# The loads of q, k and v asked for one at a time: an order of transfers on one queue of a fused attention and expert kernel

## Chip, core and metric

The kernel runs on one core of a Trainium2 chip. The metric is the device time in microseconds (us) of one execution, and lower is better. The core has five engines with their own instruction streams: PE multiplies matrices, DVE and ACT work on tiles elementwise, POOL does elementwise work and indirect transfers, and SP here only issues direct transfers (DMAs) between HBM and on-chip memory.

## What is computed

The input is q, k and v of 8 batches, 8 heads, 576 positions and 64 columns. Two attentions are added, one over means of four neighbours and one over a band of seven positions, and the sum goes through a layer of eight experts of which each token takes one:

```python
q_d, k_d, v_d = (x.reshape(B, H, S // 4, 4, D).mean(axis=3) for x in (q, k, v))
out = np.repeat(sm_attn(q_d, k_d, v_d), 4, axis=2)          # sm_attn: softmax(q k^T / 8) v
mask = np.abs(pos[:, None] - pos[None, :]) < 4
out += softmax(np.where(mask, q @ k^T / 8, -1e9)) @ v
x = out as 4608 tokens of 512;  e = argmax(x @ w_gate + modality_bias[modality_id])
result[token] = p_e * (relu(x[token] @ w1[e]) @ w2[e])
```

## The kernel before

The attention stage runs in 32 steps, step n being two pairs of heads of batch n // 4. A table, `PHASE` (line 61), gives each operation of a step a position in units of a step: operation x of step n stands at n + PHASE[x]. `build` collects all of them as calls with a position (`call`, line 1250), sorts them (line 1346) and writes them out in that order under a manual schedule, so that every engine gets its instructions in the order of the positions. A step lasts some 7 us.

Loads are calls in the same list. `load_qk` (line 226) fills a tile `qt` and a tile `kt` for half a batch, that is for the steps 2h and 2h + 1 of half h; each tile is rotated over three buffers, and each is filled by two transfers of 288 KB (line 244). The first three halves use another layout (lines 237 and 239). PE reads the tiles first in the transposes `tp` (line 298) at position 2h. The call stands at 2h - 5 + 0.4 (line 1274), just behind the transposes of step 2h - 5, the last readers of the buffer. `load_v` (line 250) fills `vw`, of which there are two, one per batch in turn. Eight transfers of 180 KB fill one: four for heads 0 to 3 (part 0) and four for heads 4 to 7 (part 4). Lines 1269 to 1272 place the two clusters of four at positions 4b + 2.84 and 4b + 3.64 for batch b + 1, those of the last batch earlier. PE reads part 0 first in `vp` (line 279) of step 4b + 4, at position 4b + 6.44, and part 4 two steps later.

All of these are issued by SP, which also issues the stores of the attention's result (`xs`, line 639, in fours) and the loads of the first expert's weights (`raw`, line 854). SP takes its instructions strictly in order. Each transfer counts up one of eight semaphores in turn, and before it issues one SP waits for the landing of the transfer eight places earlier. The first load into a reused `qt` or `kt` also waits for PE to have left the buffer, and the first of four stores for DVE. Nothing on SP waits for a time: a position is only a place in its order.

After the attention, from about 251 us, PE multiplies the tokens with the experts' weights until the end.

Of the kernel before, what the change touches and what calls it, by code (L numbers as in the profile page):

```python
# [19 lines left out]
B, H, S, D = 8, 8, 576, 64  # L20
# [31 lines left out]
NHOLD = 8  # L52

QUADS = 3


SPLIT = {4: (2, 1, 1), 2: (2,), 1: (2,)}
# [141 lines left out]
class Attention:  # L199
# [23 lines left out]
        for j in range(2):  # L223
            (nc.vector, nc.gpsimd)[j].memset(s.vw[j], 0.0)

    def load_qk(s, b, half):
        nc = s.nc

        qt = s.ld.tile([128, 9, 2, D], F32, name="qt", bufs=3)
        kt = s.ld.tile([128, 9, 2, D], F32, name="kt", bufs=3)  # L230
        s.QK[2 * b + half] = (qt, kt)
        if 2 * b + half < QUADS:
            for g in (0, 2, 1):
                for t, src in ((qt, s.q), (kt, s.k)):
                    h = src[b, 4 * half : 4 * half + 4].rearrange("(a y) s d -> a (y s) d", a=2)
                    if g == 2:
                        nc.sync.dma_start(t[:, 4], h[:, 512:640].rearrange("a p d -> p a d"))
                    else:
                        nc.sync.dma_start(s.quads(t, g), h[:, 640 * g : 640 * g + 512].rearrange("a (p x) d -> p a (x d)", x=4))
            return  # L240
        for t, src in ((qt, s.q), (kt, s.k)):
            for a in range(2):
                h = src[b, 4 * half + 2 * a : 4 * half + 2 * a + 2].rearrange("h s d -> (h s) d")
                nc.sync.dma_start(t[:, :, a], h.rearrange("(j p) d -> p j d", p=128))

    def quads(s, t, g):

        return t[:, 5 * g : 5 * g + 4].rearrange("p j a d -> p (j a d)").rearrange("p (a x) -> p a x", a=2)

    def load_v(s, b, part, W=4):  # L250
        nc = s.nc
        vw = s.vw[b % 2]


        vf = s.v.rearrange("b h s d -> (b h s) d")
        N = H * NB
        for j in (0, 2, 1, 3):
            lo = S * H * b + SUB * j - PAD
            n0, n1 = NB * part, NB * part + NB * W
            if lo + n0 * BLK < 0:  # L260
                nc.sync.dma_start(vw[PAD:KEYS, 0], vf[0 : KEYS - PAD])
                n0 = 1
            if lo + n1 * BLK > B * H * S:
                n1 = N - 1
                t = lo + n1 * BLK
                nc.sync.dma_start(vw[32 * j : 32 * j + min(KEYS, B * H * S - t), n1], vf[t : min(t + KEYS, B * H * S)])
            nc.sync.dma_start(vw[32 * j : 32 * j + KEYS, n0:n1],
                              vf[lo + n0 * BLK : lo + n1 * BLK].rearrange("(n x) d -> x n d", x=BLK)[:KEYS])
# [17 lines left out]
    def tp(s, n, nm):  # L286

        src = s.QK[n // 2]["qk".index(nm)]
        p = s.t["tp", nm, n] = s.ps.tile([128, 512], F32, name="tp", tag="T", bufs=TB)
        if n // 2 < QUADS:  # L290
            t = s.quads(src, n % 2)
# [786 lines left out]
class Large:  # L1078
# [4 lines left out]
    W = {"1": (0, 0), "2": (0, 1), "5": (1, 0), "6": (1, 0), "7": (1, 0), "4": (1, 1), "3": (0, 1)}  # L1083
# [117 lines left out]
def build(tc, q, k, v, mid, w_gate, bias, w1, w2, out):  # L1201
    nc = tc.nc
    with ExitStack() as ctx:
# [10 lines left out]
        with ExitStack() as actx:  # L1214
# [7 lines left out]
            at = Attention(tc, actx, ectx, C, ps, q, k, v)  # L1222
# [27 lines left out]
            def call(at, f, *args):  # L1250
                calls.append((at, len(calls), f, args))
# [3 lines left out]
            last = max(P["tpq"], P["tpk"], P["tpt"])  # L1255
            used = max(P["avl0"], P["avl1"])
# [3 lines left out]
            for nm, p in P.items():  # L1260
                f, i = (nm[:-1], int(nm[-1])) if nm[-1].isdigit() and nm not in ("ch1", "ch2") else (nm, 0)
# [6 lines left out]
            for b in range(B):  # L1268
                if b + 1 < B:
                    for j in range(2):  # L1270
                        late_ = (1.39, 0.78)[j] if b == B - 2 else 0
                        call(4 * b - 1 + used + 0.3 + 0.8 * j - late_, at.load_v, b + 1, 4 * j)
            for h in range(3, N // 2):
                call(2 * h - 5 + last + 0.25, at.load_qk, h // 2, h % 2)


            for j in range(3):
# [51 lines left out]
            T, R, E, W = {}, {}, {}, []  # L1329
            t = 4 * (EB - 1) + max(P[x] for x in P if x[:2] == "st") + 0.02  # L1330
# [46 lines left out]
            with tc.high_priority():  # L1377
                last = range(B - 2, B)
# [194 lines left out]
        with tc.For_i(0, nu, 1) as iv:  # L1573
# [7 lines left out]
            W = [moe.chunk(e, c) for c in range(8)]  # L1581
# [31 lines left out]
```

## Time and profile before

| | us |
|---|---|
| median of 3 runs | 666.24 |
| lowest and highest | 661.93 and 669.0 |
| the profiled execution | 670.8 |
| its span, first to last instruction | 669.1 |

The profiled execution lasts 1.7 us longer than its span. PE is busy for 634.6 us of the span (95%), DVE for 439.7, ACT for 386.9 and POOL for 340.9. A busy share is an average over stages of different kinds, so the stages have to be read apart.

### The profile page before, as it was taken

The page shows a single profiled execution, that of the slowest core. Times are in us where ns is not written, and L with a number is a line of the kernel's source. Part 1 is how long each engine was busy: PE and PEld are TensorE (multiplying, and loading weights), DVE is VectorE, ACT ScalarE, POOL GpSimd, SP SyncE. Part 2 cuts the span into 40 slices and gives each one's busy share as a digit, 9 for nine tenths or more (in the row PEclk, how much of TensorE's full clock was granted, in tenths as well). Part 3 has the DMA queues.
Part 4 walks back from the last instruction along what each step waited for, and adds up shares of the span by engine and source line. Part 5 has one row for each costly group of instructions (what it writes and reads, how often), then busy time and mean ns, then how long its engine had stood idle before and what let it go on. Part 6 is the DMA issues. An engine that isn't in the chain of part 4 may idle for free. (4 is left out here: it accounts for less than half of the span.)

```text
span 669.1 us, 16362 instructions
## 1 busy us (share of the span) xinstructions
PE 634.6 (95%) x6099; PEld 498.9 (75%) x6099; DVE 439.7 (66%) x912; ACT 386.9 (58%) x870; POOL 340.9 (51%) x378
## 2 busy tenths in 40 slices
PE   8889999998999979999999999999999999999995
PEld 5666666766676656887888788888888888889794
DVE  7678898989989685853356672758548765236610
ACT  4688889987998883313454732448144473245610
POOL 7533646635565963245059776498774820141211
PEclk9799999998999999999999999999999999999999
DMA  7999997899778924379112425134341335449300
GB/s 187 201 185 193 168 183 139 178 196 175 172 153 168 188 88 157 77 138 235 43 45 94 107 83 161 49 103 107 97 148 68 102 95 161 146 135 287 135 14 31
DMA packets 168859, 90.21 MB, mean 135 GB/s; under 512 B 131812, under 2 KB 153354, under 8 KB 168778
## 3 DMA queue, kind: packets, MB, share of 16 engines
q1 hardware_dynamic: 160810, 69.96, 48.2%
q0 software_dynamic: 7968, 19.18, 9.2%
q8 instruction: 49, 0.80, 0.6%
q14 instruction: 32, 0.26, 0.2%
HBM read 69.86 MB, written 19.51 MB: 134 GB/s over the span
## 5 line engine op out<-in xcount | busy, mean ns | idle before, releaser
L1062 PE MATMUL l<-V,H 128*128 128x512 f32 x792 | 187.2, 394 | 0.0
L1062 PEld LDWEIGHTS l<-V,H 128*128 128x128 f32 x792 | 148.0, 188 | 33.9
L948 POOL DMA_INDIRECT xg<-xs,m x64 | 76.2, 1191 | 19.2 <-issue 18.9
L426 POOL TENSOR_TENSOR le<-le,zr 128x384 f32<-128x384 f32 x32 | 26.6, 830 | 93.6 <-DVE zr L422 42.2
L1072 POOL DMA_INDIRECT out_dram<-o,tq x24 | 27.8, 1157 | 76.8 <-ACT o L1064 52.1
L442 ACT COPY Pw<-lt 32x288 f32<-32x288 f32 x128 | 54.7, 427 | 6.9 <-DVE lt L437 5.0
L1008 PE MATMUL l<-X,H 128*128 128x512 f32 (+1 forms) x240 | 54.2, 375 | 0.5 <-ACT o L1064 0.5
L1064 ACT ACTIVATE o<-l,tq 128x512 f32<-128x512 f32 x24 | 16.5, 689 | 60.9 <-issue 27.6
L645 POOL DMA_INDIRECT tab<-ig,si x36 | 36.3, 1007 | 28.5 <-DVE mni L667 21.7
L1008 PEld LDWEIGHTS l<-X,H 128*128 128x128 f32 x240 | 41.5, 188 | 9.0 <-ACT o L1064 1.0
L1165 ACT ACTIVATE H<-o 128x512 fp32r<-128x512 f32 x36 | 22.8, 634 | 39.0 <-DVE o L1187 30.4
L481 PE MATMUL avl<-Pw,vw 128*64 128x96 f32 x768 | 40.2, 251 | 5.5 <-ACT Pw L442 4.5
L331 ACT COPY kT<-tp 64x512 f32<-64x512 f32 x64 | 37.1, 580 | 7.2 <-PE tp L294 3.0
L481 PEld LDWEIGHTS avl<-Pw,vw 128*64 128x64 f32 x768 | 33.4, 136 | 10.5 <-ACT Pw L442 6.2
L1014 DVE SCALAR_TENSOR_TENSOR H<-l,H 128x512 fp32r<-128x512 f32 x24 | 16.2, 687 | 34.8 <-ACT H L1013 31.4
L885 DVE TENSOR_TENSOR V<-raw,V 128x1024 fp32r<-128x1024 f32 x22 | 32.9, 1520 | 7.7 <-ACT V L879 6.8
L412 ACT ACTIVATE de<-scd,dm 128x144 f32<-128x144 f32 x96 | 36.1, 379 | 1.9
L1072 POOL DMA_INDIRECT out_dram<-o,tg x10 | 11.3, 1133 | 50.7 <-ACT o L1064 35.7
L373 PE MATMUL sc<-kT,qT 128*24 128x64 f32 x1536 | 35.8, 226 | 0.8 <-ACT kT L331 0.8
L373 PEld LDWEIGHTS sc<-kT,qT 128*24 128x24 f32 x1536 | 25.1, 105 | 14.4 <-issue 10.3
L1013 ACT ACTIVATE H<-l 128x512 fp32r<-128x512 f32 x24 | 13.8, 596 | 35.6 <-PE l L1008 25.4
L492 DVE TENSOR_TENSOR X<-avl,Od 128x224 f32<-128x224 f32 (+1 forms) x64 | 26.5, 430 | 7.4 <-PE avl L481 2.5
(283 smaller groups left out, 1444.2 us busy)
## 6 DMA issues: line engine op xcount, KB each, us to landing
raw<-in_moe_w_dram SPq DMA_DIRECT2D x112, 128.0 KB
raw<-in_moe_w_dram SPq DMA_DIRECT2D x28, 512.0 KB
vw<-in_v_dram SPq DMA_DIRECT2D x60, 180.0 KB
qt<-in_q_dram SPq DMA_DIRECT2D x26, 288.0 KB
kt<-in_k_dram SPq DMA_DIRECT2D x26, 288.0 KB
xs<-R SPq DMA_DIRECT2D x48, 128.0 KB
xs<-G SPq DMA_DIRECT2D x16, 128.0 KB
qt<-in_q_dram SPq DMA_DIRECT2D x6, 256.0 KB
```

Of the source, the lines that this page charges most:

```text
L331: s.nc.scalar.copy(s.kB[r, g, a, PAD + 64 * g : PAD + 64 * g + 512], p[r])
L373: s.nc.tensor.matmul(p[32 * j : 32 * j + SUB, 2 * i : 2 * i + 2, :], qT[:, q0 : q0 + SUB], kB[:, :, q0 : q0 + WIN], start=False, stop=(i = ...
L412: s.nc.scalar.activation(x, s.t["scd", n][:, c].rearrange("p (k x) -> p k x", k=NB), AF.Exp, bias=m[:, c : c + 1], accum_out=s.t["z", n][: ...
L426: s.nc.gpsimd.tensor_tensor(e, e, z[:, : 2 * NB].unsqueeze(2).broadcast_to([128, 2 * NB, WIN]), op=ALU.mult)
L442: s.nc.scalar.copy(s.Pw[n % NPW][r, :, j, :SUB], s.t["lt", n][r, :, :SUB])
L481: s.nc.tensor.matmul(p[64 * a : 64 * a + 64, c], vw[:, NB * (4 * (hp // 2) + hp % 2 + 2 * a) + k, :], Pw[:, 2 * k + a], start=True, stop=T ...
L645: i = nc.gpsimd.indirect_dma_start(out=s.tab[:, :], out_offset=bass.IndirectOffsetOnAxis(ap=C.si[:, t : t + 1], axis=0), in_=C.ig[:, t, :] ...
L885: (nc.gpsimd if turn == 4 else nc.vector).tensor_tensor(lo, raw, hi.bitcast(F32), op=ALU.subtract)
L948: s.nc.gpsimd.indirect_dma_start(out=R[l].rearrange("p h (i x) -> p (h i) x", i=4)[:, i, :], out_offset=None, in_=s.xs.rearrange("n (a x) ...
L1008: nc.tensor.matmul(p[:, f % n, :], a[:, fs], x[:, k, :N], start=(k == 0 and i == 0), stop=(k == 3 and i == 2))
L1062: nc.tensor.matmul(p, l, x[:, f % 2, :], start=(f == 0 and i == 0), stop=(f == 7 and i == 2))
L1072: nc.gpsimd.indirect_dma_start(out=s.out[:, :], out_offset=bass.IndirectOffsetOnAxis(ap=T[:, h, 0:1], axis=0), in_=o, in_offset=None, boun ...
```

## The change

The four transfers of a half of q and k become four calls, half a step apart, in the order q, k, q, k of their index `part` taken as (first pair of q, second pair of q, first of k, second of k). v's eight transfers become eight calls: 0.4 of a step apart, with the second four 1.6 steps behind the first four, so that all eight are evenly spaced. For the last batch v's positions stay. The first transfer of each group keeps its position, and the tiles, the sizes and every other engine's order stay as they were.

```diff
+QKGAP, VGAP = 0.5, (0.4, 1.6)
...
+        if part:
+            return s.load_heads(b, half, part)
...
-        for t, src in ((qt, s.q), (kt, s.k)):
-            for a in range(2):
-                h = src[b, 4 * half + 2 * a : 4 * half + 2 * a + 2].rearrange("h s d -> (h s) d")
-                nc.sync.dma_start(t[:, :, a], h.rearrange("(j p) d -> p j d", p=128))
+        s.load_heads(b, half, 0)
+
+    def load_heads(s, b, half, part):
+
+        a, x = part % 2, part // 2
+        h = (s.q, s.k)[x][b, 4 * half + 2 * a : 4 * half + 2 * a + 2].rearrange("h s d -> (h s) d")
+        s.nc.sync.dma_start(s.QK[2 * b + half][x][:, :, a], h.rearrange("(j p) d -> p j d", p=128))
...
-    def load_v(s, b, part, W=4):
+    def load_v(s, b, part, W=4, js=(0, 2, 1, 3)):
...
-        for j in (0, 2, 1, 3):
+        for j in js:
...
-                        call(4 * b - 1 + used + 0.3 + 0.8 * j - late_, at.load_v, b + 1, 4 * j)
+                        for i, x in enumerate((0, 2, 1, 3)):
+                            call(4 * b - 1 + used + 0.3 + (0.8 if b == B - 2 else VGAP[1]) * j - late_ + (0 if b == B - 2 else VGAP[0]) * i,
+                                 at.load_v, b + 1, 4 * j, 4, (x,))
             for h in range(3, N // 2):
-                call(2 * h - 5 + last + 0.25, at.load_qk, h // 2, h % 2)
+                for i in range(4):
+                    call(2 * h - 5 + last + 0.25 + QKGAP * i, at.load_qk, h // 2, h % 2, i)
```

Only SP's order changes. In the middle of the stage, round the loads of half 12 (`qt_2907`, `kt_2908`) and of v for batch 5 (`vw1`), SP has this before:

```order
L267 DMA vw1_155<-in_v_dram 30x24x64 x4
L639 DMA xs_66<-R_2600 32x8x128 x4
L244 DMA qt_2907<-in_q_dram 128x9x64 x2
L244 DMA kt_2908<-in_k_dram 128x9x64 x2
L267 DMA vw1_155<-in_v_dram 30x24x64 x4
L639 DMA xs_66<-R_3029 32x4x128 x4
L639 DMA xs_66<-R_2823 32x8x128 x4
```

And this now (`qt_2905`, `kt_2906`; lines six higher):

```order
L273 DMA vw1_155<-in_v_dram 30x24x64
L250 DMA qt_2905<-in_q_dram 128x9x64
L273 DMA vw1_155<-in_v_dram 30x24x64
L250 DMA qt_2905<-in_q_dram 128x9x64
L273 DMA vw1_155<-in_v_dram 30x24x64
L250 DMA kt_2906<-in_k_dram 128x9x64
L273 DMA vw1_155<-in_v_dram 30x24x64
L645 DMA xs_66<-R_3022 32x4x128 x4
L273 DMA vw1_155<-in_v_dram 30x24x64
L645 DMA xs_66<-R_2822 32x8x128 x4
L250 DMA kt_2906<-in_k_dram 128x9x64
L273 DMA vw1_155<-in_v_dram 30x24x64
```

Two loads of v have moved in among those of q and k, and the second transfer of k has moved behind eight stores. Near the end of the stage, the loads of the last half 15 (`qt_3896`, `kt_3897`) stand, before the change, ahead of the second chunk of weights (`raw0`; the rows ISA work out an address):

```order
L244 DMA qt_3896<-in_q_dram 128x9x64 x2
L244 DMA kt_3897<-in_k_dram 128x9x64 x2
L267 DMA vw1_155<-in_v_dram 30x24x64 x4
L854 ISA
L854 DMA raw0_3709<-in_moe_w1_dram 32x1024
L854 ISA
L854 DMA raw0_3709<-in_moe_w1_dram 32x1024
L854 ISA
L854 DMA raw0_3709<-in_moe_w1_dram 32x1024
L854 ISA
L854 DMA raw0_3709<-in_moe_w1_dram 32x1024
L267 DMA vw1_155<-in_v_dram 30x24x64
```

Now only one transfer of q is left there, and the last transfer of v for batch 6 (`vw0`) comes behind four of batch 7 (`vw1`):

```order
L250 DMA qt_3895<-in_q_dram 128x9x64
L273 DMA vw1_155<-in_v_dram 30x24x64 x4
L273 DMA vw0_154<-in_v_dram 30x24x64
L250 DMA qt_3895<-in_q_dram 128x9x64
L860 ISA
L860 DMA raw0_3703<-in_moe_w1_dram 32x1024
L860 ISA
L860 DMA raw0_3703<-in_moe_w1_dram 32x1024
L860 ISA
```

The two transfers of k for half 15 (`kt_3896`) come after the weights, and the second of them after v's second part for batch 7:

```order
L250 DMA kt_3896<-in_k_dram 128x9x64
L273 DMA vw1_155<-in_v_dram 30x24x64
L272 DMA vw1_155<-in_v_dram 30x64
L273 DMA vw1_155<-in_v_dram 30x23x64
L272 DMA vw1_155<-in_v_dram 30x64
L273 DMA vw1_155<-in_v_dram 30x23x64
L272 DMA vw1_155<-in_v_dram 27x64
L273 DMA vw1_155<-in_v_dram 30x23x64
L250 DMA kt_3896<-in_k_dram 128x9x64
L645 DMA xs_66<-R_3844 32x8x128 x4
```

The second transfer of k has moved behind the weights and all of v, to just ahead of the stores.

## Rows read from the trace of the kernel before

**Rows 1.** Busy time by stage; the columns stand in its first line.

```profile
core 0: us, PE busy (x) PEld busy (x) DVE busy (x) ACT busy (x) POOL busy (x), PEclk, DMA share, GB/s
...
33.50:234.20 200.70, 185.22 (x3508) 135.22 (x3504) 172.94 (x497) 176.24 (x525) 110.92 (x147) 0.98 0.93 175
...
251.00:669.10 418.10, 408.28 (x1941) 333.71 (x1940) 229.01 (x337) 177.79 (x254) 198.10 (x170) 1.00 0.40 113
```

**Rows 2.** The waits of PE in 33.5 to 234.2 us.

```profile
PE tp L298 <- ACT PdT L459: 4.8, 10, 2.0
PE pdt L451 <- DVE eexcl L687: 1.7, 1, 1.7
...
PE cp L657 <- DMA qt<-in_q_dram: 0.9, 1, 0.9
```

**Rows 3.** The same view of DVE, and the second wait in the timeline.

```profile
DVE X L492 <- remote: 2.3, 1, 2.3
DVE lm L380 <- remote: 2.2, 1, 2.2
...
232.01 0.56 DVE L380 TENSOR_REDUCE lm<-sc 128x12 f32<-128x384 f32 x1 [2.16 <-remote]
```

**Rows 4.** Timeline of SP, 136 to 214 us (start, duration, what, count).

```profile
137.64 3.84 SPq L267 DMA_DIRECT2D vw<-in_v_dram  x4
141.58 3.92 SPq L639 DMA_DIRECT2D xs<-R  x4
145.60 1.43 SPq L244 DMA_DIRECT2D qt<-in_q_dram  x2
147.14 4.27 SPq L244 DMA_DIRECT2D kt<-in_k_dram  x2
151.45 3.51 SPq L267 DMA_DIRECT2D vw<-in_v_dram  x4
155.06 6.61 SPq L639 DMA_DIRECT2D xs<-R  x8
161.77 1.13 SPq L244 DMA_DIRECT2D qt<-in_q_dram  x2
...
194.21 2.27 SPq L244 DMA_DIRECT2D qt<-in_q_dram  x2
196.57 3.43 SPq L244 DMA_DIRECT2D kt<-in_k_dram  x2
200.06 5.63 SPq L267 DMA_DIRECT2D vw<-in_v_dram  x4
205.89 2.44 SPq L854 DMA_DIRECT2D raw<-in_moe_w_dram  x4
...
212.60 0.54 SPq L267 DMA_DIRECT2D vw<-in_v_dram  x1
```

**Rows 5.** Timeline of SP, 100 to 132 us.

```profile
100.88 1.10 SPq L244 DMA_DIRECT2D qt<-in_q_dram  x2
...
114.16 4.44 SPq L639 DMA_DIRECT2D xs<-R  x4
118.69 1.16 SPq L244 DMA_DIRECT2D qt<-in_q_dram  x2
...
127.52 4.81 SPq L639 DMA_DIRECT2D xs<-R  x4
```

**Rows 6.** The queue's own waits, 33.5 to 234.2 us, the longest of L244.

```profile
SPq L244 <- PE scd L399: 4.6, 4, 2.2
```

**Rows 7.** Timeline of PE at the first uses of loads.

```profile
167.75 1.04 PE L279 MATMUL vp<-vw,pool 128*32 128x256 f32 x12
...
180.59 0.66 PE L298 MATMUL tp<-ident,kt 128*128 128x128 f32 x4
...
209.85 1.04 PE L279 MATMUL vp<-vw,pool 128*32 128x256 f32 x12
...
221.94 0.66 PE L298 MATMUL tp<-ident,kt 128*128 128x128 f32 x4
```

**Rows 8.** Durations (ns min/median/max) by line, 33.5 to 234.2 us.

```profile
L481 PE MATMUL avl<-Pw,vw x648: 243/246/298, 37.7 to 227.2; 128*64 128x96 f32 x162
...
L331 ACT COPY kT<-tp x56: 577/580/582, 34.4 to 232.7; 64x512 f32<-64x512 f32 x56
...
L385 DVE TENSOR_TENSOR le<-sc,lm x28: 541/547/548, 36.2 to 233.9; 128x384 f32<-128x384 f32 x28
```

**Rows 9.** Busy time in three stretches round a stop of PE.

```profile
46.50:48.50 2.00, 0.02 (x1) 0.00 (x0) 2.00 (x6) 1.88 (x8) 0.00 (x0) 1.00 0.84 158
48.50:52.50 4.00, 3.99 (x45) 2.29 (x47) 2.18 (x6) 3.82 (x10) 2.41 (x4) 0.57 0.92 185
52.50:56.00 3.50, 3.50 (x81) 2.81 (x79) 2.34 (x8) 2.37 (x9) 0.38 (x1) 1.00 1.08 221
```

**Rows 10.** Issues by line on the page: count, KB of one.

```profile
vw<-in_v_dram SPq DMA_DIRECT2D x60, 180.0 KB
qt<-in_q_dram SPq DMA_DIRECT2D x26, 288.0 KB
kt<-in_k_dram SPq DMA_DIRECT2D x26, 288.0 KB
```

**Rows 11.** Timeline of SP, then of PE, round the first reused loads.

```profile
39.20 2.98 SPq L244 DMA_DIRECT2D kt<-in_k_dram  x2
...
50.44 1.93 PE L279 MATMUL vp<-vw,pool 128*32 128x256 f32 x12
```

More of the change, by code (lines that the diff above doesn't have):

```diff
@@ L224, in __init__, with load_qk @@
             (nc.vector, nc.gpsimd)[j].memset(s.vw[j], 0.0)
-    def load_qk(s, b, half):
+    def load_qk(s, b, half, part=None):
         nc = s.nc
+        if part:
+            return s.load_heads(b, half, part)
         qt = s.ld.tile([128, 9, 2, D], F32, name="qt", bufs=3)
```

## The prediction

> **What bounds the kernel now.** I read the busy time by stage first, since the change touches only transfers of the attention stage. From 33.5 to 234.2 us PE is busy for 185.2 of 200.7 us, ACT for 176.2 and DVE for 172.9 [rows 1]. Three engines are nearly full at once, and PE idles 15.5 us. The stage behind it, 418 us long with PE busy for 408 of them, is not touched. The transfers are dense too: the DMA engines have a share of 0.93 at 175 GB/s in the attention, against 0.40 behind it [rows 1].
>
> Then the waits of PE: does it ever wait for a load? The longest of its waits in this stage is for ACT's copy PdT, 4.8 us in ten pieces. One wait names a transfer, 0.9 us ahead of cp, whose matmul reads no load [rows 2]. So no row shows a load of q, k or v that came late. DVE has two odd waits, 2.3 and 2.2 us, whose releaser is only called remote [rows 3]; what held them I can't tell.
>
> Third, SP's timeline. From 137.64 to 161.77 us its rows last 3.84 + 3.92 + 1.43 + 4.27 + 3.51 + 6.61 = 23.6 of 24.1 us [rows 4]. SP issues all the time and is held by two things. One is the rule of the program that eight transfers are in flight at most. The other is the release of a buffer, of which the longest row is 4.6 us in four pieces [rows 6]. A position in the list is no time for SP. It takes the next transfer as soon as these waits allow.
>
> **The change part by part.** Nothing is removed or added: the same transfers of the same sizes move, and the orders of PE, ACT, DVE and POOL stay. So the sum has four terms.
>
> First, waits for loads that could go. At most the 0.9 us of cp [rows 2], which reads none of them. I take 0 and keep 0.9 as the end.
>
> Second, contention that could ease. If dense transfers slowed the engines, the same operation would last longer in one place than in another. It does not: over the whole stage avl lasts 243 to 298 ns with a median of 246, the copy kT 577 to 582, the subtraction le 541 to 548 [rows 8]. That excludes a gain inside instructions. Between them, the two remote waits are the nearest rows: 2.3 + 2.2 = 4.5 us [rows 3]. The second ends at 232.01 us [rows 3], behind the last load of q, k and v, where SP's order has not changed. I take 0 and keep 4.5 as the end.
>
> Third, loads that land later. From a load to the ninth transfer of the queue, which reuses its slot, bounds its landing. Between 100.88 and 114.16 that is 13.3 us, the longest I read, and between 118.69 and 127.52 it is 8.8, the shortest [rows 5]. In the middle of the stage the second k of half 12 moves behind two loads of v and eight stores, to just ahead of the load now issued at 161.77 [rows 4]. With 13.3 us it has landed at 175.1, and PE reads it at 180.59 [rows 7]: 5.5 us to spare. The fourth v of batch 5 moves behind two loads of q, to about 147.1 [rows 4], lands by 160.4 and is read at 167.75 [rows 7]: 7.3 us to spare. Most other batches and halves are placed like these. They cost nothing; what hides them is the two to four steps of work between request and first use.
>
> Three places are tighter. At the start, the fourth v of batch 1 moves to where the first k of half 4 is issued, 39.2 us at the latest. It lands between 48.0 and 52.5, and PE reads it at 50.44 [rows 11]: up to 2.1 us late. Near the end, the last v of batch 6 now comes behind one q and four v, to about 200.06 [rows 4]. It lands between 208.9 and 213.4, read at 209.85 [rows 7]: up to 3.5 late. The second k of half 15 takes the place of the transfer issued at 212.60 [rows 4], lands between 221.4 and 225.9 and is read at 221.94 [rows 7]: up to 4.0 late. The reuse of a slot is a late mark, though. By bytes, the last v of batch 6 has itself, a q and five v in flight at most, 288 + 6 x 180 KB [rows 10], some 1.4 MB, and at 175 GB/s [rows 1] that is 8.0 us: landed at 208.1, with 1.7 to spare. The second k of half 15 has itself, the other k and some 720 KB of v, 1.3 MB and 7.4 us: landed at 220.0, with 1.9 to spare. The measured rate is the nearer row, so I take 0, and keep 2.1 + 3.5 + 4.0 = 9.6 us as the end.
>
> Fourth, SP itself. The loads that move behind a load of q now share its wait for PE, the longest row being 4.6 us over four waits [rows 6], and those behind stores share theirs for DVE. It is the same queue with the same waits, and no engine but PE reads what it brings. 0.
>
> The sum is 0. The profiled execution of 670.8 us stays at 670.8; it lies 4.6 us above the median of 666.24 and 1.8 above the highest run, so about 666 us is what a median should show.
>
> **The rivals.** A, faster: crowding costs more than I can see, and half of PE's 15.5 us of idle time [rows 1] goes when loads no longer come in fours. 666.2 - 7.7 = 658.5 us. For it speak a DMA share near 1 and two waits without a named cause. Against it, the waits that can be named lead to ACT and DVE, and durations are flat.
>
> B, slower: the loads at the three tight places come late. It decides once a landing takes more than 10 us behind its request there. Each stop has a second price. After the stop of 2.0 us at 46.5 PE's granted clock was 0.57 for the next 4 us, part of them at the lower of its two levels, 1.2 GHz, before it was back at 2.4 [rows 9]; that is up to 4 x 0.43 = 1.7 us. Three stops at the late ends make 9.6 + 5.1 = 14.7 us. Half of it, 7.4 us, is the rival's price: 673.6 us. For it speaks that the last loads move most, to within 10 us of their use. Against it speak the bytes above.
> The Trainium skill, in "DMA: Bandwidth & Descriptors", section "Rules for kernel authors", says to issue a transfer early and wait on it late. By that rule alone the change is a step back, since each moved load is asked for later and none earlier than its group was. Rows of this case bear it out only where the time to spare runs out.
>
> C, nothing is spread: SP holds its queue full, so half a step in the list is no half step on the clock, and the transfers run as densely as before in another order. The time is that of the forecast, 666 us, but a reader of the trace would find the DMA share and the spacing unchanged. For it speaks that SP has nearly no gaps [rows 4].
>
> **How the numbers follow.** The forecast and C have the same time and together 0.62. A has 0.20 and B 0.18: A and B are about as likely, A slightly more as two waits are unexplained, B less as it needs landings beyond what the bytes give. The forecast's own range is that of the runs, 662 to 669. The low end of the whole range is A's 658.5 rounded down to 658, the high end B's 673.6 rounded up to 674. They leave out worse cases of A and B, under 2 in 10 together. One per cent, 6.7 us, is about what a measurement of this kernel can tell from no change. A lies below it and B above it, so faster by over 1% has 0.20, within 1% 0.62, slower 0.18.
>
> **What would show it.** Right: PE's busy time in the attention within 2 us of 185, the stage within 3 us of 200.7, no wait of vp or tp that names a load, and SP's rows as dense as before with single loads of v among those of q and k. A would show as a shorter stage with the remote waits gone, B as a stop of PE ahead of vp near 50 or 210 us, or of tp near 222 us, with the granted clock low behind it. I am wrong if the stage changes by more than 6.7 us with no such wait, or if the stage behind 251 us changes at all.

## The result and the profile after

The changed kernel takes 674.59 us in the median of 4 runs (672.21 to 677.37), beside 666.73 for the kernel before (4 runs, 661.93 to 669.0). The ratio is 1.0116, with a 95% interval of 1.0076 to 1.0156. The profiled execution took 672.21 us, its span 670.5. The two profiles differ by only 1.4 us of span, since the profiled execution of before, at 670.8 us, was slower than any of its timed runs. So I look for what is new in the trace, and not for the difference of the two spans.

Busy time by stage, in the changed kernel, answers to [rows 1]:

```profile
core 0: us, PE busy (x) PEld busy (x) DVE busy (x) ACT busy (x) POOL busy (x), PEclk, DMA share, GB/s
33.50:234.20 200.70, 180.74 (x3432) 132.33 (x3429) 171.45 (x491) 173.02 (x518) 108.67 (x143) 0.97 0.96 171
251.00:669.10 418.10, 409.90 (x1965) 335.12 (x1963) 234.42 (x339) 180.85 (x260) 199.41 (x171) 1.00 0.40 113
```

In the attention PE is busy 4.5 us less than before in the same window, the DMA engines have a higher share (0.96 for 0.93), and they moved less (171 for 175 GB/s). The stage behind it is as full as it was. The waits of PE in the attention answer to [rows 2]; the columns are the total, the count and the longest:

```profile
PE tp L304 <- ACT PdT L465: 8.5, 12, 2.2
PE vp L285 <- issue: 3.5, 1, 3.5
...
PE pdt L457 <- DVE eexcl L693: 1.7, 1, 1.7
```

One line is new: a single stop of 3.5 us ahead of `vp`, which no row of before has. Its longest rival, the 2.2 us ahead of `tp`, stands beside a wait of ACT named remote, of which before has its own at the same place [rows 3]. PE's timeline around the new stop, one row for each group (start, duration, and in brackets the idle time ahead):

```profile
206.71 0.54 PE L379 MATMUL sc<-kT,qT 128*24 128x64 f32 x24
210.70 1.93 PE L285 MATMUL vp<-vw,pool 128*32 128x256 f32 x12 [3.45 <-issue]
212.56 1.23 PE L472 MATMUL avd<-PdT,vd 96*64 96x144 f32 x8
213.72 1.71 PE L405 MATMUL scd<-kd,qd 64*64 64x144 f32 x12
215.35 0.76 PE L379 MATMUL sc<-kT,qT 128*24 128x64 f32 x24
```

This is the `vp` of step 26, the first reader of the second part of v for batch 6. Before, the same group lasted 1.04 us and started without a stop at 209.85 [rows 7]. The four groups behind the stop last 1.93 + 1.23 + 1.71 + 0.76 = 5.63 us; in the steps around it they last 1.04 + 0.71 + 0.95 + 0.54 = 3.24. So the stop costs 3.45 us and another 2.4 of slow work behind it, together 5.8. The granted clock of the stretch shows why (columns as above; first the changed kernel, then the kernel before):

```profile
210.00:225.00 15.00, 13.07 (x210) 9.30 (x210) 9.54 (x24) 8.69 (x28) 9.29 (x13) 0.80 1.06 182
```

```profile
210.00:225.00 15.00, 13.81 (x266) 9.94 (x258) 12.69 (x36) 13.89 (x41) 12.56 (x16) 1.00 0.90 190
```

0.80 for 1.00: part of the window ran at the lower of the two levels, 1.2 GHz, after PE had stood still. SP's queue names the load. These rows of its timeline are the last transfer of v for batch 6 and the second k of half 15:

```profile
204.04 0.82 SPq L273 DMA_DIRECT2D vw<-in_v_dram  x1
...
216.07 2.42 SPq L250 DMA_DIRECT2D kt<-in_k_dram  x1
```

PE had nothing left ahead of `vp` at 206.71 + 0.54 = 207.25, only 3.2 us after SP issued the load. The wait is put down to "issue", so the row itself names no transfer. The semaphore events kept in the trace do: PE's queue waits on the semaphore that this load counts up until 210.64 us, and the last of the load's completions stands at 210.61. What made the load late is what the experiments had to show.

### The profile page after: what moved, and what is told of

Read it like the earlier page. It is cut to its first block, busy times and chain, and to the rows that moved or that the text cites. A ratio compares the mean times of both kernels' runs of the same rounds, so it can differ in the third digit from the quotient of the medians.

```text
span 670.5 us, 16363 instructions
## 1 busy us (share of the span) xinstructions
PE 633.2 (94%) x6099; PEld 498.5 (74%) x6099; DVE 443.5 (66%) x912; ACT 387.2 (58%) x870; POOL 339.6 (51%) x378
## 5 line engine op out<-in xcount | busy, mean ns | idle before, releaser
L891 DVE TENSOR_TENSOR V<-raw,V 128x1024 fp32r<-128x1024 f32 x22 | 35.2, 1621 | 10.2 <-ACT V L885 9.3
L1132 DVE TENSOR_TENSOR G<-X,G 128x1024 fp32r<-128x1024 f32 x15 | 23.2, 1552 | 20.9 <-ACT G L1131 20.9
```

The source lines that it names most:

```text
L891: (nc.gpsimd if turn == 4 else nc.vector).tensor_tensor(lo, raw, hi.bitcast(F32), op=ALU.subtract)
```

## The experiments

Theory L: the last loads of the stage come late, and each stop brings a stretch of low clock. Theory S: spread loads cost a little everywhere. All ratios are against the kernel before, run on the same chip in the same session, with 6 or 12 runs of each edited kernel and 23 or 29 of the kernel before. The times of SP's rows are those at which SP takes up a transfer. A row also holds the wait for a free place among the eight in flight, so it lasts from 0.3 us to, in the table below, 2.5 us.

**1. Only the end put back (e1).** `QK` stands for the positions of q and k, `V` for those of v.

```diff
-QK: QKGAP * i
+QK: (0 if h >= N // 2 - 2 else QKGAP) * i
-V: clusters if b == B - 2
+V: clusters if b >= B - 3
```

The expectations for the first four kernels:

> The changed kernel, but v of batch 6 and the halves 14 and 15 of q and k are asked for at their positions of before. Theory L (a late load near the end): the changed kernel stops 3.45 us ahead of vp of step 26 (207.25 to 210.70 us), and its clock falls for some 4 us behind it, 2.4 us more, 5.9 us together. Without the stop the kernel takes 674.6 - 5.9 = 668.7 us or less, down to 663 us where the 3 us that the changed kernel is ahead of before at 166 us are real. No wait of vp in the trace. Theory S (spacing costs everywhere: loads of v wait in the queue behind loads of q and k that wait for PE): 13 of 15 groups are spaced still, the kernel stays at 673 us or above.

Measured: 1.0043 (1.001 to 1.0076). Its profile has no late load and a span of 662.7 us. Most of the loss lies in the end, and 0.4% is left.

**2. Of the end, only v put back (e2):** `QK` as in the changed kernel, `V` clusters from `b >= B - 3`.

> The changed kernel, but only v of batch 6 is asked for at its positions of before; the halves 14 and 15 of q and k stay spaced. Theory L with v alone to blame: the same as e1_end_old, 663 to 669 us. If the second k of half 15, read at step 30, is late in some executions too, 2 to 4 us above e1_end_old. Theory S: 673 us or above.

Measured: 1.0202 (1.0158 to 1.0245), no better than the changed kernel and worse than either form of the expectation under theory L allowed. The stop has moved to the other tight place. The profiled execution, 669.34 us, is the fastest of the six, whose median is 676.12; that the others stopped for longer is likely, but no trace shows it. PE's timeline and SP's:

```profile
216.50 0.65 PE L304 MATMUL tp<-ident,qt 128*128 128x128 f32 x4
220.99 0.63 PE L304 MATMUL tp<-ident,kt 128*128 128x128 f32 x4 [3.84 <-DMA kt<-in_k_dram]
```

```profile
213.68 0.49 SPq L250 DMA_DIRECT2D kt<-in_k_dram  x1
```

Here the row names the transfer, k of half 15. Issued at 213.68, it was read at 220.99, 7.3 us later.

**3. Only v spread (e3):** `QK: 0 * i`.

> Only v is spaced, q and k are asked for at one position as before. Theory L: the last load of v for batch 6 stands at its late place, now behind all four loads of half 15, so vp of step 26 stops for 3.5 us or more: 672 to 677 us. Theory S, where spacing of either kind costs in proportion: about half of the loss, 670 us, with no single stop above 1.5 us.

Measured: 1.0104 (1.0069 to 1.0138). The last loads of v are late in three batches, named as DMA in two of the rows; the row at 178.21 (step 22) names a store `xs`, and there the load is my reading. PE, and SP's last v of batch 6:

```profile
146.28 1.06 PE L285 MATMUL vp<-vw,pool 128*32 128x256 f32 x12 [1.04 <-DMA vw<-in_v_dram]
...
178.21 1.93 PE L285 MATMUL vp<-vw,pool 128*32 128x256 f32 x12 [2.84 <-DMA xs<-R]
...
215.00 1.93 PE L285 MATMUL vp<-vw,pool 128*32 128x256 f32 x12 [8.08 <-DMA vw<-in_v_dram]
```

```profile
209.51 0.70 SPq L273 DMA_DIRECT2D vw<-in_v_dram  x1
```

**4. Only q and k spread (e4):** all of v in its old clusters.

> Only q and k are spaced, v is asked for in clusters as before. Theory L: no stop of vp, 663 to 669 us; if k of half 15 is late at step 30, up to 4 us more. Theory S: about half of the loss, 670 us.

Measured: 1.0168 (1.0121 to 1.0216). `vp` of step 26 does not stop, and the second k of half 15 is late as theory L allowed, but by far more than its 4 us. PE and SP:

```profile
225.73 1.09 PE L304 MATMUL tp<-ident,kt 128*128 128x128 f32 x4 [10.51 <-DMA kt<-in_k_dram]
```

```profile
219.29 0.49 SPq L250 DMA_DIRECT2D kt<-in_k_dram  x1
```

PE asked for the tile at 225.73 - 10.51 = 215.22 us, 4 us before SP had issued the load at all.

**5. Only the end spread (e5):** `QK: (QKGAP if h >= N // 2 - 2 else 0) * i`, `V` clusters if `b != B - 3`.

> The kernel before, in which the end alone is spread: the transfers of q and k of halves 14 and 15 half a step apart, v of batch 6 at even distances, all earlier loads as before. Late loads at the end (theory L): the second k of half 15 and the last v of batch 6 come late here as in the changed kernel, a stop of TensorE of 3 to 10 us ahead of vp near 210 us or of tp near 220 us, and a ratio of 1.006 to 1.016. Spread costs everywhere (theory S): at most 1.004, since 22 of 27 spread groups of loads are back in their clusters.

Measured: 0.9972 (0.9943 to 1.0001). Theory L's number fell: the spread end by itself costs nothing. Its traces of PE and SP show why that does not contradict the late load:

```profile
204.20 1.04 PE L285 MATMUL vp<-vw,pool 128*32 128x256 f32 x12
...
216.26 0.66 PE L304 MATMUL tp<-ident,kt 128*128 128x128 f32 x4
```

```profile
194.93 0.94 SPq L273 DMA_DIRECT2D vw<-in_v_dram  x1
...
209.88 0.50 SPq L250 DMA_DIRECT2D kt<-in_k_dram  x1
```

SP stands at the same entries of the same list, but 9.1 and 6.2 us earlier than in the changed kernel, while PE is 3 us ahead, and they go out 9.3 and 6.4 us before they are read. So the spread of the earlier loads takes part in the loss; in the changed kernel's profile SP's queue is further behind.

**6. Of the end, only q and k put back (e6).**

> The changed kernel, with the transfers of q and k of halves 14 and 15 together again and v of batch 6 spread. Theory L: the stop at tp near 220 us is gone, the one ahead of vp of step 26 stays or grows (the spread v now stands behind four transfers of half 15, asked together): 4 to 9 us of stop there, ratio 1.008 to 1.015, as with v alone spread (1.0104). If the two late loads were one and the same cause, the ratio would fall to that of the kernel with both back (1.0043).

Measured: 1.0147 (1.0098 to 1.0196). As theory L has it, the stop at `vp` stays and grows, and none is at `tp` for a load of k (the changed kernel's own profile had none there either). PE and SP:

```profile
213.39 1.93 PE L285 MATMUL vp<-vw,pool 128*32 128x256 f32 x12 [7.66 <-DMA vw<-in_v_dram]
```

```profile
208.21 0.82 SPq L273 DMA_DIRECT2D vw<-in_v_dram  x1
```

**7. All loads spread, other transfers out of their way (e8, e9).** The first two pieces of the weights go behind the second k of half 15, in the changed kernel (e8) and in the kernel before (e9):

```diff
-            for c, x in enumerate((0.2, 2.4, 3.4, 4.4)):
+            for c, x in enumerate((3.36, 3.38, 3.4, 4.4)):
```

> The changed kernel, with all loads at their spread places, but the first two pieces of the experts' weights (eight transfers, 3.27 and 3.80 us of SP's queue at 182.88 and 205.92 us) asked after the second k of half 15 and not before it. Theory L, in the form that these loads are late by what stands ahead of them in SP's queue: the last v of batch 6 goes out 3.3 us earlier (200.8 for 204.04) and the second k of half 15 7 us earlier (209 for 216.07), the stop of 3.45 us ahead of vp goes, and the ratio falls from 1.0116 to 1.000 to 1.006; the first splits of the weights, near 237 us, are not held up. Rival: the loads are late by their own spread alone, or by the sharing of the DMA engines whatever the order: 1.009 or more. Rival: the weights come late and the stop moves to the first expert: 1.009 or more, with a stop of TensorE after 237 us.

> The kernel before with the same move of the weights, as the measure for the run above. Theory L: no load of the kernel before was late at the end, so nothing is gained, 0.997 to 1.003; if the weights are late, slower by what stops after 237 us.

Measured: 1.0014 (0.9979 to 1.0049) and 0.9968 (0.9938 to 0.9999). No load of q, k or v was moved, and the loss is gone. SP's rows of e8:

```profile
197.54 1.32 SPq L273 DMA_DIRECT2D vw<-in_v_dram  x1
...
208.79 0.49 SPq L250 DMA_DIRECT2D kt<-in_k_dram  x1
```

They are issued 6.5 and 7.3 us earlier than in the changed kernel. The second is what was expected; the first is 3 us more than the one piece of weights ahead of it explains, since SP was further on before that in this execution. The price of the stop can be read here too: PE is through with the work ahead of the same `vp` at 207.19 us, for 207.25 in the changed kernel, and the span is 665.5 us for 670.5. The 5.0 us between them are near the 5.8 worked out above. Whether the weights held the loads up by their places in SP's order or by their share of the DMA engines, e8 does not separate.

**8. The changed kernel again (e10).**

> The changed kernel once more, for a second profile and a narrower interval. If its loss is the late loads at the end (theory L), the second profile shows again a stop of TensorE of 2 us or more ahead of vp of step 26 or of tp of step 30, each as long as 6.4 to 7.3 us less the time by which its load was issued ahead of need; ratio 1.008 to 1.016. If the stop of the first profile was a chance of that execution: no such stop, and a time near the same ratio all the same.

Measured: 1.0147 (1.0098 to 1.0197). The stop is there again and longer, at the same `vp`, and the load is read 7.5 us after its issue, a little past the 6.4 to 7.3 expected. Its last completion stands at 213.70 us. PE and SP:

```profile
213.79 1.93 PE L285 MATMUL vp<-vw,pool 128*32 128x256 f32 x12 [6.09 <-issue]
```

```profile
206.26 2.46 SPq L273 DMA_DIRECT2D vw<-in_v_dram  x1
```

This execution took longer than the first for another reason as well: a stop of several engines at once near 235 us, of 5.7 us at DVE, put down to remote (below).

**9. The last third put back, half the distances, both edits at 0.997 (e7, e11, e12).** e7: `h >= N // 2 - 4` and `b >= B - 4` as before. e11: `QKGAP, VGAP = 0.25, (0.2, 1.2)`. e12: the edits of e5 and e9 together.

> The changed kernel with the loads of the last third as they were (v of batches 5 and 6, q and k of halves 12 to 15), the earlier ones spread. The kernel with only the end put back (v of batch 6, halves 14 and 15) was at 1.0043. Theory: that rest is v of batch 5 and the second k of halves 12 and 13, late in some executions as in the kernel with v alone spread (2.84 us ahead of vp at 178.21 us): then 0.997 to 1.002 here. Rival: the rest is the cost of spread loads anywhere: 1.003 to 1.006, as before.

> The changed kernel with half the distances: q and k a quarter of a step apart, v 0.2 of a step and its second four 1.2 steps later for 1.6. The eighth v is then asked one step (5.5 us) earlier and the second k three quarters of a step (4 us) earlier in SP's list. Theory L: both are ahead of their need by the 6.4 to 7.3 us that they take to land, the stops go: 0.999 to 1.005. Rival S (what spreading costs grows with the distance, everywhere): 1.005 to 1.008.

> The kernel before with both edits that stood at 0.997 alone: the loads of the end spread, and the first two pieces of the weights after the second k of half 15. Theory: neither took anything from the path that sets the end, and each 0.997 is the spread of the measurement: 0.995 to 1.001, no better than either alone. Rival: each gives 0.3 per cent of its own, by freeing the DMA engines for other transfers: 0.991 to 0.995.

Measured: 1.0003 (0.9974 to 1.0031), 0.9981 (0.9944 to 1.0018) and 0.9982 (0.9943 to 1.0021). With half the distance the loss is gone, and not halved. SP's row of e11 for the last v of batch 6 stands 15.3 us before PE reads it at 209.62:

```profile
194.37 1.70 SPq L273 DMA_DIRECT2D vw<-in_v_dram  x1
```

The 0.4% left in e1 is gone in e7, which fits late loads of batch 5 and of halves 12 and 13 as in e3. But the intervals of the two overlap, and no trace of e1 shows such a load, so this stays open. e12 is no better than e5 or e9 alone, so the 0.3% of e9, whose interval ends just below 1, is not borne out as a gain of its own.

The late loads side by side, all times in us; "needed" is the start of the reader less its wait:

| kernel | load | issued | needed | read | issue to read | stop |
|---|---|---|---|---|---|---|
| changed | v, batch 6 | 204.04 | 207.25 | 210.70 | 6.7 | 3.45 |
| changed, again | v, batch 6 | 206.26 | 207.70 | 213.79 | 7.5 | 6.09 |
| v only (e3) | v, batch 6 | 209.51 | 206.92 | 215.00 | 5.5 | 8.08 |
| q, k of the end back (e6) | v, batch 6 | 208.21 | 205.73 | 213.39 | 5.2 | 7.66 |
| v of the end back (e2) | k, half 15 | 213.68 | 217.15 | 220.99 | 7.3 | 3.84 |
| q, k only (e4) | k, half 15 | 219.29 | 215.22 | 225.73 | 6.4 | 10.51 |

The stop is the time from issue to read less the lead (needed less issued) by the way the columns are made. What is measured is that this time lies between 5.2 and 7.5 us in all six, while the leads go from 3.5 us down to -4.1, and that the stops follow the leads. All six executions with such a stop belong to kernels at 1.010 to 1.020. The seven edited kernels whose profile shows no late load are at 0.997 to 1.004. That speaks for theory L against S: e8, with every load spread, leaves S at most 0.5% by its interval (its median is 0.3% above that of e9, the clustered order with the same weights). Theory L needs what e5 added to it, since in these profiles the spread end is late only where SP's queue is behind as well. The loss takes three things together: spread loads at the end (put back in e1), spread loads ahead of it (put back in e5) and the weights ahead of the last loads (moved in e8). Taking away any one removes it, but for the 0.4% of e1.

## Why the prediction was wrong

The forecast was 666 us, the measured median 674.59, above the range's end of 674. Step by step:

The first two terms stand. No wait for a load was there to be lost, and no other operation became longer or shorter (avl lasts 243 to 297 ns, kT 577 to 583, le 540 to 548). PE reads at 207.25 what it read at 209.85 before, 2.6 us earlier, but this is no gain of rival A: the first of the two remote waits of [rows 3] did not come in this execution, and it did not come in e9 either, which has the clustered loads of before.

The third term failed, at the last v of batch 6, which I had put at 0 "by bytes". The way to that number had two parts. The time from issue to landing was taken as 8.0 us, and 5.2 to 7.5 was measured: on the safe side. The lead was wrong. I read the issue time off the old timeline, 200.06 us [rows 4], against a use at 209.85 [rows 7]: 9.8 us. Measured were 204.04 and 207.25: 3.2 us. Of the 6.6 us between them 4.0 are SP's, which came to this entry later, and 2.6 are PE's, which came earlier. Both were taken from one execution as if the change and chance left them alone.

SP came later since its queue was behind in front of this entry too, a cost that the fourth term had at 0. From 33.5 to 190 us the DMA engines moved 174 to 180 GB/s in the four profiles whose middle is clustered (before, e5, e9, e12) and 163 to 174 in the ten whose middle is spread. For the changed kernel, at 169, that is 5 x 156.5 = 780 KB less than before by 190 us, or 4.5 us at 174 GB/s, beside the 4.0 that SP was late. The two fit in size. e1 and e7 bear it out, in which the same 179 transfers as before stand ahead of SP's two small transfers `tg`, only in another order: SP comes to these at 200.5 and 203.7 us, before at 192.5. With the weights behind it, the spread e8 comes to it at 190.8 and the clustered e9 and e12 at 193.4 and 191.1, so spread loads alone do not set SP back in that profile. Why SP falls behind is open, and single executions of one order differ by as much (e8 and the changed kernel, alike up to the weights, by 5.6 us at the stores near 170 us).

The lead is what the change used up. Before, SP issued the last v of batch 6 at 184.70 and the second k of half 15 at 198.75, 25 and 23 us before their use. Of this the list took 15 and 14 us by plan, and the rest had to carry the landing and SP's arrears.

Of the three tight places, the first and the third were not late in the changed kernel's own profiles: `vp` starts at 50.44 as before, and the second k of half 15 is issued 8 and 5 us before its turn, which came behind a wait of 0.8 us put down to ACT, or of 0.3 us. In e2 and e4 the third was late, so it was as tight as the prediction had it.

Rival B named the mechanism, the place and the second price, and its sign came as written: a stop ahead of `vp` near 210 us with the granted clock low behind it. Its time, 673.6, was near by an even trade: it took half of three stops, and one whole stop came, of 3.45 + 2.39 = 5.8 us in one execution and of 6.09 + 2.15 = 8.2 in the other (the groups behind it: 1.93 + 1.23 + 1.69 + 0.54 for 3.24). The condition it was given, a landing more than 10 us behind its request, was wrong: the landings took less, the requests came late. I weighed it at 0.18 since I set bytes against it, which bear on the landing only. The rule that the Trainium skill gives in "DMA: Bandwidth & Descriptors", section "Rules for kernel authors", issue early and wait late, is borne out with numbers here: in the profiles of e5 and e8 leads of 6.4 us (the second k of half 15 in e5) and of 9.3 to 10.5 us cost nothing, and the six late loads of the table had 3.5 us or less.

Rival C holds in part: SP's rows are as dense as before (they fill 90% of the time from 100 to 190 us, before 91%), but the time is not that of the forecast, though only the order differs.

## What to carry to other kernels

When a load moves back in an in-order queue, compare its lead (from issue to first use) with the time from issue to read, and leave several microseconds for the queue's own arrears: an issue time read off the old timeline is not where the moved entry will stand. Where leads shrink only at the end of a stage, look at what stands ahead of the last loads; here eight transfers of weights stood among and ahead of them, in two fours issued 50 and 27 us before any of the weights is read, and moving them away took the loss back with every load still spread. A loss that vanishes when the distance is halved is a deadline and not a rate.

## What was not expected

In the attention stage, waits that the profile calls remote come and go between executions: they stand at two moments, of 2.3 and 2.2 us, in the profile of before [rows 3], at one of 2.2 us in the changed kernel, at one of 5.7 us in its second profile, at two of 1.5 and 3.2 us in e11, and in none of the other ten. Here is the longest, in DVE's row of e10:

```profile
237.74 0.61 DVE L410 TENSOR_REDUCE dm<-scd 128x3 f32<-128x432 f32 x1 [5.74 <-remote]
```

PE stops in the midst of one group `avl` over the same microseconds. The cause was not tried. A profile with such waits is a poor base for a sum: the two of before make 4.5 us, of the 4.8 to 8.0 by which its span lies above those of e5, e9 and e12 (661.1 to 664.3), whose middle is clustered too.
